# Routing logits issued as one block, and two of the last half's first four stores issued by GpSimd

## The chip, the cores and the metric

The kernel runs on one core of one Trainium2 chip. The time is the device time of one execution in microseconds (us); of several runs the median counts. The engines are called as in the profile: PE is TensorE (PEld its weight loads), DVE is VectorE, ACT is ScalarE, POOL is GpSimd, SP is SyncE. SP, ACT and POOL also issue the DMAs, each from its own queue and in the order of its program. A "q" behind an engine's name stands for its instruction queue. L12 is line 12 of the kernel.

## The reference

Three things are computed one after the other, all in float32.

1. A polysketch attention over 4 batches, 4 heads, 1088 positions and 32 features: queries and keys are mapped to 64 products of two 8-wide sketches, and the output is `num / den` with the sums over the keys.
2. A bridge turns the output into `x`, 4352 tokens by 128 features.
3. A Sinkhorn routing over 8 experts, each a two-layer network with 1024 hidden units:

```
logits = x @ w_gate                      # 4352 x 8
P = exp(logits - logits.max())
for _ in range(8):                       # rows, then columns
    P /= P.sum(1, keepdims=True) + 1e-09
    P /= P.sum(0, keepdims=True) + 1e-09
    P *= N / E
for e in range(E):
    h = relu(x @ w1[e])
    out += P[:, e:e+1] * (h @ w2[e])
```

## The kernel before

**Layout.** Tokens lie along the free axis: `xT` holds 128 features by 4352 tokens, in four batches of 1088. The experts' networks are the bulk of the work. A matrix product is cut into blocks of 64 rows and 64 columns, with sums and differences of blocks in place of some products, seven products where eight are plain. For that the second matrices `w2` of experts 1 to 7 are brought into seven derived blocks ("forms") in DRAM first.

**Phases.** First attention, batch by batch. Then the logits, the exponential and eight Sinkhorn rounds (`routing`). Neither fills PE, so the network of the first expert, which needs no weights `P` (they are applied to its outputs later), is worked off beside them: `first` (L763, product L770 and relu L772, DVE differences L785) and `into` (L824, second product L834), with copies of finished sums on ACT (L693 to L710). At the end of `routing` the transposed `P` goes to DRAM (`pT`, L622). Then comes the weighted phase (`weighted`, L1109) for the other experts: a row of `pT` is spread over the partitions (`load_weights`, L1058, DMA L1062), POOL multiplies `xT` by it (`weigh`, L1064, L1069), SP swaps the halves (L1072), POOL and DVE make the block sums (`sum_x`, L1074, L1077), the first matrices come with `load_raw` (L952, L958), the second ones with `load_second` (L965, L972 and L975), and PE runs first products (L1156) and second products (L1309) to the end.

**What sets the order.** The stretch around the change stands in a `manual_schedule` over DVE and PE alone: on these two the instructions come in the order of the program text. ACT's, POOL's and SP's order is the scheduler's choice, except for instructions pinned with `keep_in_program_order`, which keep their order among each other. `attention` and `routing` are generators that yield amounts of fill; the driver calls `fill(n)` with each, which runs that many steps of the first expert's network. The driver (L1640 to L1647) counts the yields of `routing` from `i = 0`: at the first it takes a step of `second_forms`, up to `i = 4` it fills the whole amount at once, and from `i = 5` on it fills twice half of it and takes a step of `second_forms` behind each half. Before, the yields are 5, 0.6, 0.6, 0.6, 2.2 and then 4.25 in each of the eight Sinkhorn rounds.

**The logits.** `logits(c)` (L493) issues, for chunk `c` of 512, 288 and 288 tokens of each batch, a 32-column product per batch (L497) into one PSUM bank; `logits_turned` (L503) lets DVE transpose the bank into `lgp` (L506). The maximum over all is taken on DVE (L585), turned by PE (L589), and ACT takes the exponential (L594).

**The second forms.** `second_forms` (L991) loads the raw matrices into buffers of the early phases, then in four stages for each expert 1 to 7: `begin` negates one half on ACT (L1015) and lets SP copy four parts to DRAM (L1016, L1018, L1020, L1022; the last two read the negated half); `add_first`, `add_second` and `add_third` are accumulating DMAs issued by POOL (L1025). All are pinned. When all is issued the early pools are closed (L1650), and the pool `late`, which holds the tiles of L1062, takes their place.

**The end.** The last group of tokens is finished in two halves by `finish_last` (L1525): for `u == 0` the sum is completed on DVE (L1510 to L1523) and transposed into a tile `r`, for `u == 1` the accumulator is transposed into a tile `yt` (both L1535). `store` (L727, DMA L736) writes a half with four DMAs of 32 partitions, dealt over the queues that it is given, in turn. POOL's last arithmetic is L1437; L1698 is the end of the program, with a DRAIN on each engine and a barrier.

Of the kernel before, what the change touches and what calls it, by code (L numbers as in the profile page):

```python
# [52 lines left out]
def kernel(  # L53
# [12 lines left out]
    nc = tc.nc  # L66
# [30 lines left out]
    def bank():  # L97
        return aps.tile([P, 512], F32, tag="a", name="a")
# [394 lines left out]
    def logits(c):  # L493
        lo, hi = chunks[c]
        pg = bank()[:, 0:hi - lo]
        for b in range(B):
            nc.tensor.matmul(pg[32 * b:32 * (b + 1)], wg, xT[:, b * S + lo:b * S + hi], start=True, stop=True,  # L497
                             tile_position=(0, 32 * b))
        lgs.append((c, pg))
# [3 lines left out]
    def logits_turned():  # L503
        c, pg = lgs.pop(0)
        lo, hi = chunks[c]
        nc.vector.transpose(out=lgp[:, lo // 32:hi // 32, :].rearrange("p a e -> p (a e)"), in_=pg)  # L506
# [69 lines left out]
    def routing():  # L576

        yield 5
        for c in range(len(chunks)):
            logits(c)  # L580
            yield 0.6
            logits_turned()
        lg = lgp[:, :, 0:E]
        mx = sk.tile([P, 1], F32, tag="mx", name="mx")
        nc.vector.tensor_reduce(out=mx, in_=lg, axis=AX.XY, op=Alu.max)  # L585
        yield 2.2
        pm = bank()[:, 0:P]
        for s in range(2):
            nc.tensor.matmul(pm[64 * s:64 * (s + 1)], mx.to_broadcast([P, 64]), ident, start=True, stop=True,  # L589
                             tile_position=(0, 64 * s))  # L590
        nc.vector.reduce_max(mx, pm, axis=AX.X)
        nc.vector.tensor_scalar(mx, mx, -1.0, 64 * math.log(2.0), op0=Alu.mult, op1=Alu.add)
        pw = p2s[0]
        nc.scalar.activation(out=pw[:, :, 0:E], in_=lg, func=Act.Exp, bias=mx[:, 0:1])  # L594

        step = 1.5 * 2.0 ** (23 - 149 + 64)
        nc.vector.tensor_scalar(pw[:, :, 0:E], pw[:, :, 0:E], step, step, op0=Alu.add, op1=Alu.subtract)
        for it in range(ITERS):
            rs = sk.tile([P, SA], F32, tag="rs", name="rs")
            nc.vector.reduce_sum(rs, pw, axis=AX.X)  # L600
            nc.vector.reciprocal(rs, rs)
            p1 = p1s[it % 2]
            nc.vector.scalar_tensor_tensor(p1[:, 0:SA], rs.unsqueeze(2).to_broadcast([P, SA, E]), UP,
                                           pw[:, :, 0:E], op0=Alu.mult, op1=Alu.mult)
            cs = sk.tile([P, E], F32, tag="cs", name="cs")
            nc.vector.reduce_sum(cs, p1.rearrange("p g e -> p e g"), axis=AX.X)
            yield 4.25
            pc = bank()[:, 0:E]
            for s in range(2):
                nc.tensor.matmul(pc[64 * s:64 * (s + 1)], ones[:, 0:64], cs, start=True, stop=True,  # L610
                                 tile_position=(0, 64 * s))
            cr = sk.tile([P, E], F32, tag="cr", name="cr")
            nc.vector.reciprocal(cr, pc)
            last = it == ITERS - 1
            pw = lgp if last else p2s[(it + 1) % 2]
            nc.vector.scalar_tensor_tensor(pw[:, :, 0:E], cr.unsqueeze(1).to_broadcast([P, SA, E]),
                                           float(N) / E * (1.0 if last else UP), p1[:, 0:SA],
                                           op0=Alu.mult, op1=Alu.mult)

        nc.vector.transpose(out=lgT.rearrange("p a s -> p (a s)"), in_=lgp.rearrange("p a e -> p (a e)"))  # L620
        for b in (1, 0, 2, 3):
            nc.sync.dma_start(out=pT[:, b * S:(b + 1) * S],  # L622
                                                  in_=lgT[32 * b:32 * b + E].rearrange("p a s -> p (a s)"))
# [99 lines left out]
    def one_store():  # L723
        if stores:
            stores.pop(0)()

    def store(yt, b0, b1, queues=(nc.sync,), put_off=False):  # L727
        first, k = b0, 0
        while b0 < b1:
            b, a = divmod(b0, SA)  # L730
            m = min(b1 - b0, SA - a)
            for r in range(4):
                to = AP(tensor=out.tensor, offset=out[b * S + a, 32 * r].offset, ap=[[SA * DM, 32], [DM, m], [1, 32]])
                from_ = yt[32 * r:32 * (r + 1), b0 - first:b0 - first + m, :]
                queue = queues[k % len(queues)]
                stores.append(lambda queue=queue, to=to, from_=from_: queue.dma_start(out=to, in_=from_))  # L736
                k += 1
            b0 += m
        while stores and not put_off:
            one_store()  # L740
# [368 lines left out]
    def weighted():  # L1109
# [170 lines left out]
        def seconds(t):  # L1280
# [33 lines left out]
            if g in whole and last:  # L1314
                begin_last(g)
                for u, cols in ((0, (0, n)), (1, (0, 128)), (1, (128, n))):
                    m = 2 * u + (cols[0] > 0)
                    for k, b in enumerate(((0, 2), (3, 1))[u]):
                        for r in range(2):
                            for half in range(2):  # L1320
                                nc.tensor.matmul(  # L1321
                                    acc[g][m][H2 * half:H2 * (half + 1), cols[0]:cols[1]],
                                    raw(half, k, r), flat(h[b], n)[:, r, cols[0]:cols[1]],
                                    start=False, stop=True, tile_position=(0, H2 * half),
                                    skip_group_check=True)
                    finish_last(g, u, cols)
                yield
                yield
                return
# [161 lines left out]
        def turned_room(k, n):  # L1491
            t = late[0].tile([P, NW], F32, tag="yt", name="yt", bufs=1)[:, 0:n] if k else room("r", n)
            return t.rearrange("p (b d) -> p b d", d=32)
# [9 lines left out]
        def last_of(g, u):  # L1503
            lo, n, es = wgroups[g]
            return lo + n * (1 - u), n

        def add_sum(g, m, u, cols):
            at, n = last_of(g, u)
            y = kept[0][:, at + cols[0]:at + cols[1]]
            nc.vector.tensor_tensor(y, acc[g][m][:, cols[0]:cols[1]], y, op=Alu.add)  # L1510
# [14 lines left out]
        def finish_last(g, u, cols):  # L1525
            at, n = last_of(g, u)
            if cols[0] == 0:
                ends[g, u] = turned_room(u, n)
            yt = ends[g, u]
            y = kept[0][:, at:at + n]  # L1530
            if u:
                y = acc[g][2 + (cols[0] > 0)][:, cols[0]:cols[1]]
            else:
                add_sum(g, 0, 0, cols)
            nc.vector.transpose(out=yt[:, cols[0] // 32:cols[1] // 32].rearrange("p b d -> p (b d)"), in_=y)  # L1535
            if cols[1] == n:
                store(yt, at // 32, (at + n) // 32, (nc.sync, nc.scalar))

        behind = (x for at in range(len(todo)) for x in seconds(at))
        for t in range(len(todo)):  # L1540
# [60 lines left out]
    with tc.manual_schedule(engines={engines.DVE, engines.PE}):  # L1601
# [38 lines left out]
        for i, n in enumerate(routing()):  # L1640
            if i == 0:
                next(made)
            for _ in range(2 if i > 4 else 0):
                fill(n / 2)
                next(made, None)
            if i < 5:
                fill(n)  # L1647
# [55 lines left out]
```

## Time and profile before

| | |
|---|---|
| median of 3 runs | 882.61 us (882.1 to 882.68) |
| profiled execution | 881.87 us |
| its span | 880.1 us |
| mean granted TensorE clock | 1.0 |
| PE busy | 874.7 us (99%) |
| DVE busy | 724.0 us (82%) |
| ACT busy | 386.8 us (44%) |
| POOL busy | 261.8 us (30%) |
| DMA | 149.06 MB, mean 169 GB/s |

The span is the time from the first to the last recorded instruction; the execution's own time lies 1.77 us above it. PE counts as busy while its pipelined matmuls are modelled to run. Idle time of an engine that others don't wait for costs nothing, so for DVE, ACT and POOL the timelines around a wait say more than these shares. In the rows below, a row of a timeline has start, duration, engine, line, operation, output and inputs, the count of instructions put together, and in brackets the idle time ahead of it with what ended it; a row of the chain of waits has start, duration and what stood on the chain.

### The profile page before, as it was taken

The numbers are of one execution on the slowest core, as the hardware profiler recorded it, in microseconds if no ns is written. First come the engines' busy times: TensorE is split into PE (matmuls) and PEld (weight loads), VectorE is DVE, ScalarE is ACT, GpSimd is POOL, SyncE is SP. The second block draws the span as 40 slices with busy tenths as digits, with TensorE's granted clock in tenths as the row PEclk, the third lists the DMA queues.
The fourth block names the chain that finished last, engine by engine and source line by source line (L and its number), as shares of the span: only waits on it lengthen the run. The fifth ranks groups of instructions, "written<-read, shape, count | busy, mean of one in ns | idle before, by whom it ended". The sixth has DMA issues, their size and how long they took to land.

```text
span 880.1 us, 26108 instructions
## 1 busy us (share of the span) xinstructions
PE 874.7 (99%) x10792; PEld 600.0 (68%) x10792; DVE 724.0 (82%) x982; ACT 386.8 (44%) x801; POOL 261.8 (30%) x254
## 2 busy tenths in 40 slices
PE   9999999999999999999999999999999999999998
PEld 6788656878775666666666666666555555557776
DVE  8699689978888877777887778888788888888897
ACT  3455557544444433333343333334343344444442
POOL 3131126354433323222222222221323323312431
PEclk9999999999999999999999999999999999999999
DMA  8888399796766554444435544434755557567662
GB/s 262 269 287 267 91 220 257 119 263 193 209 189 205 165 164 121 142 135 130 126 100 138 143 123 126 119 111 111 193 152 148 153 139 218 151 153 220 215 198 49
DMA packets 120887, 149.06 MB, mean 169 GB/s; under 512 B 52289, under 2 KB 79809, under 8 KB 120385
## 3 DMA queue, kind: packets, MB, share of 16 engines
q1 hardware_dynamic: 112656, 136.92, 54.8%
q0 software_dynamic: 6720, 10.19, 5.8%
q8 instruction: 85, 1.39, 0.6%
q10 hardware_dynamic: 1392, 0.28, 0.2%
q14 instruction: 34, 0.27, 0.1%
HBM read 104.86 MB, written 25.99 MB: 149 GB/s over the span
## 4 chain that ended last, share of the span: by engine, by line
PE 99%; DMA 0%; DVE 0%; SPq 0%; issue 0%; DVEq 0%
PE pair L1156 39%; PE s L1309 39%; PE a L770 9%; PE s L834 7%; PE a L336 1%; PE a L465 1%; DMA kx<-in_k_dram 0%; PE a L306 0%; PE s L375 0%; PE a L429 0%; PE s L395 0%; PE a L497 0%; PE s L1321 0%; PE a L375 0%; PE a L395 0%; PE a L610 0%
## 5 line engine op out<-in xcount | busy, mean ns | idle before, releaser
L1156 PE MATMUL pair<-xf,w1x 64*64 64x320 f32 (+3 forms) x4496 | 552.1, 466 | 0.0
L1309 PE MATMUL s<-hb,w 64*64 64x480 f32 (+3 forms) x2544 | 354.2, 466 | 0.0
L1156 PEld LDWEIGHTS pair<-xf,w1x 64*64 64x64 f32 x4496 | 258.7, 133 | 110.3 <-ACT hb L1169 0.9
L1172 DVE CUSTOM_DVE_ANT_0 hb<-pair,copies 128x960 f32<-128x960 f32 (+3 forms) x234 | 214.8, 918 | 100.7 <-PE pair L1156 89.7
L1309 PE MATMUL s<-hb,ws 64*64 64x480 f32 (+3 forms) x1888 | 274.5, 468 | 0.0
L1309 PEld LDWEIGHTS s<-hb,w 64*64 64x64 f32 x2544 | 153.1, 133 | 63.4 <-ACT turn L1362 0.4
L1309 PEld LDWEIGHTS s<-hb,ws 64*64 64x64 f32 x1888 | 115.0, 133 | 47.2 <-DVE hb L1221 0.6
L1069 POOL TENSOR_TENSOR xf<-xT,pb 128x960 f32<-128x960 f32 (+3 forms) x40 | 70.1, 1755 | 240.4 <-ACT turn L1362 184.1
L1077 POOL TENSOR_TENSOR xf<-xf 128x960 f32<-128x960 f32 (+3 forms) x39 | 68.4, 1753 | 225.3 <-ACT turn L1362 159.9
L1169 ACT ACTIVATE hb<-pair 128x640 f32<-128x640 f32 (+3 forms) x86 | 66.4, 772 | 148.4 <-PE pair L1156 148.4
L770 PE MATMUL a<-xT,w 128*64 128x416 f32 (+3 forms) x512 | 122.7, 464 | 0.0
L772 ACT ACTIVATE hb<-a 128x416 f32<-128x416 f32 (+3 forms) x128 | 59.5, 468 | 57.1 <-PE a L770 51.7
L1214 DVE TENSOR_TENSOR hb<-hb 128x960 f32<-128x960 f32 (+3 forms) x78 | 75.7, 971 | 7.5 <-PE pair L1156 0.5
L1362 ACT COPY turn<-s 128x1 f32<-128x1 f32 x134 | 20.9, 156 | 138.7 <-PE s L1309 138.7
L1221 DVE TENSOR_TENSOR hb<-hb 128x960 f32<-128x960 f32 (+3 forms) x78 | 72.4, 928 | 8.1 <-DVE hb L1218 0.9
L1217 DVE TENSOR_TENSOR hb<-hb 128x960 f32<-128x960 f32 (+3 forms) x78 | 76.4, 979 | 2.6 <-ACT hb L1169 0.8
L1250 ACT COPY copies<-pair 128x960 f32<-128x960 f32 (+3 forms) x78 | 59.8, 767 | 35.5 <-PE pair L1156 35.4
L1246 ACT COPY copies<-pair 128x960 f32<-128x960 f32 (+3 forms) x78 | 60.0, 769 | 33.1 <-PE pair L1156 33.1
L1241 ACT COPY copies<-pair 128x960 f32<-128x960 f32 (+3 forms) x78 | 59.8, 767 | 33.1 <-PE pair L1156 29.2
L834 PE MATMUL s<-hb,ws 128*64 128x416 f32 (+3 forms) x224 | 71.6, 474 | 0.0
L1218 DVE TENSOR_TENSOR hb<-hb 128x960 f32<-128x960 f32 (+3 forms) x78 | 71.4, 915 | 0.0
L770 PEld LDWEIGHTS a<-xT,w 128*64 128x64 f32 x512 | 54.5, 137 | 19.0 <-issue 7.2
(206 smaller groups left out, 662.4 us busy)
## 6 DMA issues: line engine op xcount, KB each, us to landing
w1x<-w1x SPq DMA_DIRECT2D x87, 256.0 KB, 4.0
w<-w2x SPq DMA_DIRECT2D x71, 256.0 KB, 3.1
ws<-w2x SPq DMA_DIRECT2D x35, 256.0 KB, 3.5
pb<-pT SPq DMA_DIRECT2D x14, 480.0 KB, 4.2
xf<-xf SPq DMA_DIRECT2D x28, 240.0 KB, 3.1
w1x<-w1x SPq DMA_DIRECT2D x7, 896.0 KB, 6.2
ws<-w2x SPq DMA_DIRECT2D x36, 128.0 KB, 3.4
pb<-pT SPq DMA_DIRECT2D x13, 320.0 KB, 4.4
```

The costliest lines, as they stand in the source:

```text
L770: nc.tensor.matmul(ph[sl], loaded_w[j][0][:, P * f + H2 * s:P * f + H2 * (s + 1)], xT[:, at + lo:at + hi], start=True, stop=True, tile_pos ...
L834: nc.tensor.matmul(sums[g][i][H2 * s:H2 * (s + 1)], w, x, start=c == 1, stop=c == per, tile_position=(0, H2 * s))
L1069: nc.gpsimd.tensor_tensor(xf[:, 0:2].rearrange("p b n -> p (b n)"), xT[:, lo:lo + 2 * n], weights.pop(i), op=Alu.mult)
L1077: nc.gpsimd.tensor_tensor(xf[:, 4:6], xf[:, 1:4:2], xf[:, 0:2], op=Alu.subtract)
L1156: nc.tensor.matmul(out[H2 * col:H2 * (col + 1), r], w1[rows, PLACE[form], o:o + H2], xf[rows, x], start=start, stop=stop, tile_position=(H ...
L1169: nc.scalar.activation(out=x, in_=y, func=Act.Relu)
L1172: nc.vector._custom_dve(TENSOR_ADD_SAT, out=flat(out, n), in0=x, in1=flat(y, n), s0=math.inf, s1=0.0)
L1214: nc.vector.tensor_tensor(ts[0], h[3], h[0], op=Alu.subtract)
L1217: nc.vector.tensor_tensor(ts[1], h[3], h[1], op=Alu.subtract)
L1218: nc.vector.tensor_tensor(ts[2], h[1], ts[0], op=Alu.subtract)
L1221: nc.vector.tensor_tensor(ts[3], h[2], ts[2], op=Alu.subtract)
L1309: nc.tensor.matmul(out_[H2 * half:H2 * (half + 1)], w[rows], flat(x, n)[rows, r], start=c == 1, stop=True, tile_position=(H2 * rho, H2 * h ...
```

## The change

Two places. In `routing` the three `logits` are issued one right behind the other; the transposes of the first two chunks follow at once, then the fill of 0.6, then the third transpose. The fill that stood between the chunks (0.6 each) is added to the one behind the maximum, so that the sum is as before (4.0 up to L589): 0.6 three times and 2.2 become 0.6 and 3.4. So `routing` yields three times instead of five ahead of the Sinkhorn rounds. In `finish_last` the four stores of the half `u == 0` are dealt over SP, ACT, POOL, POOL instead of SP, ACT, SP, ACT; those of `u == 1` stay. Lines behind L582 are two further down in the changed kernel.

```
@@ routing
         for c in range(len(chunks)):
             logits(c)
-            yield 0.6
-            logits_turned()
+        logits_turned()
+        logits_turned()
+        yield 0.6
+        logits_turned()
         lg = lgp[:, :, 0:E]
         mx = sk.tile([P, 1], F32, tag="mx", name="mx")
         nc.vector.tensor_reduce(out=mx, in_=lg, axis=AX.XY, op=Alu.max)
-        yield 2.2
+        yield 3.4
@@ finish_last
             if cols[1] == n:
-                store(yt, at // 32, (at + n) // 32, (nc.sync, nc.scalar))
+                store(yt, at // 32, (at + n) // 32, (nc.sync, nc.scalar) if u else (nc.sync, nc.scalar, nc.gpsimd, nc.gpsimd))
```

## The prediction

> **What bounds the kernel now.** I read the page first, then the chain of waits.
>
> ```profile
> span 880.1 us, 26108 instructions
> PE 874.7 (99%) x10792; PEld 600.0 (68%) x10792; DVE 724.0 (82%) x982; ACT 386.8 (44%) x801; POOL 261.8 (30%) x254
> PE 99%; DMA 0%; DVE 0%; SPq 0%; issue 0%; DVEq 0%
> ```
>
> PE is busy in 874.7 of 880.1 us and makes up 99% of the chain that ended last. So there is next to nothing to win: a gain needs fewer PE microseconds or a shorter tail behind PE. There is much to lose: whatever makes PE wait is added in full. I therefore read three places: PE around the logits, the stretch between the logits and the first weighted product (which engine waits for what), and the last ten microseconds. The profiled execution took 881.87 us, 1.77 more than its span; the median of the three runs shown is 882.61, so I add 0.74 to whatever the sum gives.
>
> **Part 1: the logits on PE.** The timeline of PE (start, duration, line, operation, count):
>
> ```profile
> 107.60 0.51 PE L834 MATMUL s<-hb,ws 128*64 128x416 f32 x1
> 108.04 1.06 PE L497 MATMUL a<-xT,wg 128*32 128x512 f32 x8
> 109.04 0.92 PE L770 MATMUL a<-xT,w 128*64 128x416 f32 x4
> 109.79 0.87 PE L834 MATMUL s<-hb,w 128*64 128x416 f32 x4
> 110.58 1.18 PE L497 MATMUL a<-xT,wg 128*32 128x288 f32 x16
> 111.69 0.92 PE L770 MATMUL a<-xT,w 128*64 128x416 f32 x4
> ```
>
> and two rows of the chain:
>
> ```profile
> 169.82 0.35 PE a L770 x2
> 187.38 5.54 PE pair L1156 x80
> ```
>
> Two 64-column matmuls side by side with 416 columns take 0.35 us. By columns, a wave of four 32-column logit matmuls takes 0.43 at 512 and 0.24 at 288. From 107.60 to 111.69 are 4.09 us; the work in them is 0.35 (the last L834) + 0.86 (chunk 0, two waves) + 0.70 + 0.70 (the FFN step between) + 0.97 (chunks 1 and 2, four waves) = 3.58. The 0.51 left are four changes between 32- and 64-column tiles, 0.13 each at most (some of it is the half step by which the L834 are offset). The FFN step now comes behind all three chunks, so two changes go: **-0.2 us**, bounds 0 and -0.5. The fill time taken from here is put behind the reduction (2.2 to 3.4), so PE's work up to the maximum stays the same.
>
> DVE's turns of the logits, before:
>
> ```profile
> 111.29 1.07 DVE L506 STREAM_TRANSPOSE kT<-a 128x512 f32<-128x512 f32 x2
> 112.76 0.47 DVE L506 STREAM_TRANSPOSE kT<-a 128x288 f32<-128x288 f32 x1
> ```
>
> The first two, 1.07 us together, now stand ahead of two L785 and an L683 instead of behind them, where the logits of chunks 0 and 1 are complete at about 109.0 and 109.6. PE would wait if it wanted a bank that DVE hasn't read, or the relu that L785 makes: both come a step (four L770, four L834: 1.4 us) later, and each turn takes half a microsecond. I cost it at nothing; uncovered, it would be the 1.07.
>
> **Part 2: what the change moves without naming it.** The driver of `routing` counts its yields: from the sixth on (`i > 4`) it fills in two halves and takes a step of `second_forms` behind each. Before, five yields stand ahead of the Sinkhorn rounds (5, three of 0.6, 2.2), so the forms begin in the first round. Now there are three (5, 0.6, 3.4), so `i` is 3 and 4 in the first two rounds, and the forms begin **two rounds later**; ten steps at two a round still fit into the six rounds left. The order of the changed program's instructions agrees: ahead of ACT's first negation (L1015) now stand seven relus (L772), a group of part copies (L693 to L710) and two relus more, where it was two relus behind the exponential. Two rounds by L610, a product that each has once, are 12.9 us:
>
> ```profile
> 122.44 0.29 PE L610 MATMUL a<-cs,ones 128*64 128x8 f32 x4
> 135.30 0.23 PE L610 MATMUL a<-cs,ones 128*64 128x8 f32 x2
> ```
>
> and by ACT's order the new place of the first negation is the one right behind the two relus at 133.87:
>
> ```profile
> 120.32 0.62 ACT L1015 ACTIVATE halves<-halves 128x512 f32<-128x512 f32 x1
> 133.87 0.93 ACT L772 ACTIVATE hb<-a 128x416 f32<-128x416 f32 x2
> 140.21 0.62 ACT L1015 ACTIVATE v<-v 128x512 f32<-128x512 f32 x1
> ```
>
> So the first negation goes from 120.32 to about 134, **13 to 14 us later**, and the last from 140.21 to about 154. Behind it hang SP's queue, in order, and POOL's accumulate DMAs (L1025), in order:
>
> ```profile
> 117.94 1.08 SPq L1018 DMA_DIRECT2D w2x<-halves  x1
> 120.96 0.37 SPq L1020 DMA_DIRECT2D w2x<-halves  x1
> 151.34 0.74 SPq L1022 DMA_DIRECT2D w2x<-v  x1
> 172.06 1.35 SPq L622 DMA_DIRECT2D pT<-qT  x4
> 175.75 0.83 SPq L1062 DMA_DIRECT2D pb<-pT  x2
> 181.32 1.17 SPq L1072 DMA_DIRECT2D xf<-xf  x2
> ```
>
> ```profile
> 123.41 2.19 POOL L1025 DMA_DIRECT2D w2x<-halves  x2 [22.19 <-DMA w2x<-halves]
> 165.26 0.89 POOL L1025 DMA_DIRECT2D w2x<-v  x1 [0.90 <-DMA w2x<-v]
> 179.76 1.54 POOL L1069 TENSOR_TENSOR xf<-xT,pb 128x640 f32<-128x640 f32 x1 [9.97 <-DMA pb<-pT]
> ```
>
> SP's L1020 waits for the first negation: behind 117.94 it sits until 120.96, which is 120.32 + 0.62. The chain ends with the accumulate of form 7 issued at 165.26; it reads a buffer of the early pools, and L1062, the first load into the late pool that takes their place, waits for it. Landing times of L1025 (minimum, median, maximum):
>
> ```profile
> DMA to landing us min/median/max: 3.4/7.1/10.3
> ```
>
> At the minimum it lands at 168.7. L1062 was issued at 175.75 on account of L622, so the chain had 7.1 us of **cover**. PE's first weighted product (L1156, 187.38) needs L1069, and the second, one step of 0.54 later at 187.92, needs the swap DMAs of L1072, issued from 181.32 to 182.5, which land
>
> ```profile
> DMA to landing us min/median/max: 2.6/2.6/2.6
> ```
>
> after issue: the path from the issue of L1062 to this product is 8.8 us long (175.75 to 184.5). So there is a second cover of 187.92 - 184.5 = 3.4 us. Does the chain shift by the full two rounds? The row of the stretch from 118 to 160 says what limits it:
>
> ```profile
> 118.00:160.00 42.00, 42.00 (x269) 28.01 (x267) 38.24 (x75) 28.04 (x59) 20.77 (x21) 1.00 1.12 242
> ```
>
> (the last two columns are DMA share and GB/s). From 118 to 160 the transfers fill the engines, and each form is issued two rounds late besides, so the chain runs faster only where emptier engines let its tail catch up. I take a shift of 13.5 us, between 12 and 15. Form 7 lands at 182.2, L1062 goes out at 182.7 (I allow 0.5 for the wait itself), and the second product can start at 191.5 to 191.9. PE is there at 187.92 - 0.2 = 187.7. **Stall: +4.0 us**; 2.3 at a shift of 12, 6 at 15, and nothing if the chain makes up 4 us of its delay. The next loads are pushed by the same 7 us, of which PE's own delay of 4 covers the larger part; the rest of 3 us they have:
>
> ```profile
> 182.60 1.01 SPq L972 DMA_DIRECT2D w<-w2x  x2
> 192.92 0.61 PE s L1309 x8
> ```
>
> L972 goes out 10.3 us ahead of the L1309 that reads it. So I add nothing more for them. From there the loop is PE bound as before and gives nothing back.
>
> **Part 3: the end.** Two of the four stores of the first half (`r`, L736) go from SP and ACT to POOL. The tail before, one row each of the timelines of SP (twice), DVE and POOL, and the landing times of all L736:
>
> ```profile
> 875.63 0.82 SPq L736 DMA_DIRECT2D out_dram<-r  x2
> 876.54 0.91 SPq L736 DMA_DIRECT2D out_dram<-yt  x2
> ```
>
> ```profile
> 876.06 0.28 DVE L1535 STREAM_TRANSPOSE yt<-s 128x96 f32<-128x96 f32 x1 [0.26 <-PE s L1321]
> ```
>
> ```profile
> 872.96 0.66 POOL L1437 TENSOR_TENSOR w<-w,m 64x224 f32<-64x224 f32 x1
> ```
>
> ```profile
> DMA to landing us min/median/max: 1.6/1.7/1.8
> ```
>
> The last transpose ends at 876.34 and the second half's first store goes out at 876.54, behind the two `r` stores: 0.2 us to save, if those stores alone set the end. What POOL itself does at the end stands in the view of the kernel's last line, L1698:
>
> ```profile
> L1698 POOLq DRAIN  x3: 46/102/5527, 872.9 to 879.8; - x3
> L1698 SPq DRAIN  x3: 7/7/7, 879.3 to 879.6; - x3
> ```
>
> POOL's first drain starts at 872.9 and takes 5.53 us: it ends at 878.4, 4.8 us behind the end of L1437 (873.6), though POOL has nothing left to do. No other engine has this: SP's take 7 ns. Now it is hidden, with 0.9 us to spare, because SP's first drain, the last to come, is at 879.3. In the changed kernel POOL's stores stand ahead of the drain. They wait for the `r` transpose, as the store at 875.63 does, and take on POOL what plain copies from POOL took at L489 (issue about 0.56 us each), with landings of
>
> ```profile
> DMA to landing us min/median/max: 2.4/2.5/2.6
> ```
>
> The second ends issuing at about 876.75 and lands by 878.8, no later than the `yt` stores now, the last of which goes out at about 877.0 and lands 1.6 to 1.8 us later; at L1025's fastest, 3.4, it would land at 879.6. The drain then ends at 876.75 + 4.8 = 881.6 instead of 878.4, and the barrier behind it goes from 879.3 to 881.6: **+2.3 us**, and the 0.2 of part 3 is hidden. Bounds: -0.2 if the drain's length belongs to a moment and not to what precedes it, +3 if it grows with the two stores.
>
> The Trainium skill, "DMA: Bandwidth & Descriptors", section "SWDGE vs HWDGE vs iDMA", says that plain transfers go to SP or ACT and only accumulating, casting or irregular ones to GpSimd: it speaks against this edit. By the fixed 2.0 us of its section "Anatomy of one DMA" the estimate for the second POOL store would be landed by about 878.7, and the end would not move; neither section has a price for the drain, which is what I count.
>
> **Sum.** -0.2 + 4.0 + 2.3 = +6.1 on 881.87, so 888.0; with 0.74, **888.7 us**.
>
> **The rivals.**
> - *Stall, but the drain stays hidden* (0.20): 881.87 - 0.2 - 0.2 + 4.0 + 0.74 = 886.2. For it: the profile doesn't say what the drain waits for. Against it: it starts the moment POOL is free, and nothing else ends at 878.4.
> - *Drain, but the forms catch up* (0.15): a shift under 10 us stays under 7.1 + 3.4 us of cover less the 0.5; some rest of the stall, 0.3, gives 881.87 - 0.2 + 0.3 + 2.3 + 0.74 = 885.0. For it: with the first negations late, the early transfers run in emptier engines.
> - *Not slower* (0.05): the cover at the start of the weighted phase swallows the delay of the forms. It decides at the same 10 us of shift, and needs the drain hidden as well; then only the two savings are left: 881.87 - 0.4 + 0.74 = 882.2, within the bound of no change. More than 0.4 us can't be won, since PE's other work is the same.
> - *The forms collide* (0.08): the last accumulate now runs beside L622 and lands at the slow end, 10.3 instead of 3.4; L1062 goes 5 to 7 us later still: +5 on the sum, 893.7.
>
> **How the numbers follow.** The forecast (stall and drain) has 0.52. Its own range, by the bounds of the shift, is 887.0 to 890.7. The range for 8 in 10 takes in the rival without the drain and most of the one without the stall: 884.3 to 890.6. 0.2% is 1.8 us, about what a measurement of this kernel can tell from no change. Faster by more than that: 0.03, for no row gives more than 0.4; within: 0.05; slower: 0.92.
>
> **What would show it.** Changes of tile near 108 to 111: two, not four. No step of the forms in the first two Sinkhorn rounds, the first negation at about 134 and the last at 154; the accumulate of form 7 near 179; L1062 at about 182 and released by that DMA; a gap on PE between the first and the second weighted product near 188 to 192, four microseconds long; POOL's long drain starting behind the `r` stores and ending at the span's end less 0.7. I am wrong if L1062 goes out near 176, if PE's busy share stays as it is, or if POOL's drain is short.

## The result and the profile after

The changed kernel takes 891.77 us in the median of 4 runs (891.44 to 892.77), the kernel before 882.36 (881.54 to 882.68): +9.4 us, ratio 1.011 with a 95% interval of 1.0092 to 1.0127. The forecast was 888.7, +6.1, with a range that ended at 890.6. The profiled execution of the changed kernel took 891.44 us with a span of 889.7. From its page:

```profile
span 889.7 us, 26109 instructions
PE 876.2 (98%) x10792; PEld 601.7 (68%) x10792; DVE 724.2 (81%) x982; ACT 387.2 (44%) x801; POOL 262.7 (30%) x256
PE 96%; DMA 2%; DVE 0%; POOL 0%; issue 0%; POOLq 0%; SPq 0%; DVEq 0%; ACT 0%; ACTq 0%
```

PE is busy 1.5 us longer with the same 10792 instructions, and the span grew by 9.6: PE stands still for longer, and something made the same matmuls slower. The three places that the prediction named show it one after the other. First PE around the logits:

```profile
107.82 0.51 PE L836 MATMUL s<-hb,ws 128*64 128x416 f32 x1
108.27 2.04 PE L497 MATMUL a<-xT,wg 128*32 128x512 f32 x24
110.23 0.92 PE L772 MATMUL a<-xT,w 128*64 128x416 f32 x4
110.98 0.87 PE L836 MATMUL s<-hb,w 128*64 128x416 f32 x4
111.68 0.87 PE L772 MATMUL a<-xT,w 128*64 128x416 f32 x4
```

One block of 24. From the last L836 ahead of it to the second L772 behind it are 3.86 us, where the same work took 4.09: 0.23 won, as forecast. Next the forms and the first weighted load, from the timelines of SP and POOL:

```profile
117.79 1.01 SPq L1020 DMA_DIRECT2D w2x<-halves  x1
134.27 0.37 SPq L1022 DMA_DIRECT2D w2x<-halves  x1
181.92 0.83 SPq L1064 DMA_DIRECT2D pb<-pT  x2
188.81 1.17 SPq L1074 DMA_DIRECT2D xf<-xf  x2
```

```profile
177.89 0.89 POOL L1027 DMA_DIRECT2D w2x<-v  x1 [0.83 <-DMA w2x<-v]
187.26 1.53 POOL L1071 TENSOR_TENSOR xf<-xT,pb 128x640 f32<-128x640 f32 x1 [4.74 <-PE s L836]
```

SP stands from 118.8 to 134.27, until the first negation is done, and the accumulate of form 7 comes at 177.89 instead of 165.26, 12.6 us later. L1064 (L1062 before) goes out at 181.92 instead of 175.75. The bracket at L1071 names PE, whose matmuls end every 0.35 us; the load that L1071 needs, the first `pb`, landed 5.0 us behind its issue (3.7 before), just ahead of it. PE at that place, and its granted clock by stretches of 1 us (the third column from the right, ahead of DMA share and GB/s):

```profile
190.66 1.35 PE L1158 MATMUL pair<-xf,w1x 64*64 64x320 f32 x8 [3.46 <-DMA w1x<-in_moe_w_dram]
192.87 6.49 PE L1158 MATMUL pair<-xf,w1x 64*64 64x320 f32 x72 [0.86 <-DMA xf<-xf]
```

```profile
192.00:193.00 1.00, 0.14 (x5) 0.14 (x6) 0.00 (x0) 0.00 (x0) 1.00 (x2) 0.63 1.01 373
193.00:194.00 1.00, 1.00 (x10) 0.62 (x14) 0.00 (x0) 0.00 (x0) 0.90 (x2) 0.50 0.92 320
...
195.00:196.00 1.00, 1.00 (x16) 0.68 (x12) 0.00 (x0) 0.05 (x1) 0.00 (x0) 0.66 0.98 199
196.00:197.00 1.00, 1.00 (x22) 0.57 (x18) 0.10 (x1) 0.70 (x1) 0.00 (x0) 1.00 0.95 261
```

The brackets are the two waits, 3.46 us ahead of the first product and 0.86 ahead of the second. The first product waited for its own weights, the load L960 behind L1064 in SP's queue, which landed 7.1 to 7.4 us after issue where it had been 5.4 to 5.5; the second waited for the halves that L1074 swaps. The second product starts at 192.87, where it was 187.92: **+4.95 us**. Behind it the clock reads 0.50, and the 72 matmuls take 6.49 us; before, 80 took 5.54, so 72 took 4.99: **+1.5 us**. Last, the end: POOL's stores, the last transpose, and the drains.

```profile
882.58 1.32 POOL L738 DMA_DIRECT2D out_dram<-r  x2 [2.29 <-DVE yt L1537]
```

```profile
882.73 0.28 DVE L1537 STREAM_TRANSPOSE yt<-s 128x96 f32<-128x96 f32 x1 [0.26 <-PE s L1323]
```

```profile
L1700 POOLq DRAIN  x3: 46/102/5820, 883.1 to 889.4; - x3
L1700 SPq DRAIN  x3: 7/7/7, 886.1 to 889.1; - x3
```

POOL's long drain starts at 883.1 and ends at 888.9; SP is done at 886.1 and waits for it. From the end of the last transpose to the end of the span are now 6.7 us (883.01 to 889.7) where there were 3.76 (876.34 to 880.1): **+2.9 us**. The parts 4.95 (in which the 0.2 won at the logits is contained), 1.5 and 2.9 make 9.35 of the span's 9.6; the rest is spread over the weighted phase.

### The profile page after: what moved, and what is told of

Read it like the earlier page. It is cut to its first block, busy times and chain, and to the rows that moved or that the text cites. A ratio compares the mean times of both kernels' runs of the same rounds, so it can differ in the third digit from the quotient of the medians.

```text
span 889.7 us, 26109 instructions
## 1 busy us (share of the span) xinstructions
PE 876.2 (98%) x10792; PEld 601.7 (68%) x10792; DVE 724.2 (81%) x982; ACT 387.2 (44%) x801; POOL 262.7 (30%) x256
## 4 chain that ended last, share of the span: by engine, by line
PE 96%; DMA 2%; DVE 0%; POOL 0%; issue 0%; POOLq 0%; SPq 0%; DVEq 0%; ACT 0%; ACTq 0%
PE pair L1158 39%; PE s L1311 38%; PE a L772 9%; PE s L836 7%; DMA qx<-in_q_dram 1%; PE a L465 1%; PE a L336 1%; DMA v<-in_v_dram 0%; DMA xf<-xf 0%; PE a L429 0%; PE a L306 0%; PE s L395 0%; DMA raw<-in_S_dram 0%; PE a L497 0%; POOL xf L1071 0%; DVE kT L289 0%
## 5 line engine op out<-in xcount | busy, mean ns | idle before, releaser
L1071 POOL TENSOR_TENSOR xf<-xT,pb 128x960 f32<-128x960 f32 (+3 forms) x40 | 70.5, 1763 | 234.4 <-ACT turn L1364 182.8
L772 PE MATMUL a<-xT,w 128*64 128x416 f32 (+3 forms) x512 | 121.7, 464 | 0.0
L836 PE MATMUL s<-hb,ws 128*64 128x416 f32 (+3 forms) x224 | 70.9, 474 | 0.0
L772 PEld LDWEIGHTS a<-xT,w 128*64 128x64 f32 x512 | 52.1, 137 | 23.0 <-issue 11.0
```

Of the source, the lines that this page charges most:

```text
L772: nc.tensor.matmul(ph[sl], loaded_w[j][0][:, P * f + H2 * s:P * f + H2 * (s + 1)], xT[:, at + lo:at + hi], start=True, stop=True, tile_pos ...
L836: nc.tensor.matmul(sums[g][i][H2 * s:H2 * (s + 1)], w, x, start=c == 1, stop=c == per, tile_position=(0, H2 * s))
L1071: nc.gpsimd.tensor_tensor(xf[:, 0:2].rearrange("p b n -> p (b n)"), xT[:, lo:lo + 2 * n], weights.pop(i), op=Alu.mult)
```

## The experiments

The theory, from the two traces: three independent things happen. The block of logits wins a little; the forms begun two Sinkhorn rounds late make PE wait and then run at half the clock; the two stores on POOL push its drain out. The rivals: that the block costs by itself; that it takes block and late forms together; that the stores count only by their landing.

**Each part alone.** Four kernels on one chip. The two stores on the kernel before:

```
-  store(yt, at // 32, (at + n) // 32, (nc.sync, nc.scalar))
+  store(yt, at // 32, (at + n) // 32, (nc.sync, nc.scalar) if u else (nc.sync, nc.scalar, nc.gpsimd, nc.gpsimd))
```

> The kernel before with the two GpSimd stores alone. Theory (POOL's long drain starts behind its last instruction and is pushed out by the stores): +2.9 us on before, as the tail of the changed kernel grew from 3.76 us behind the last transpose to 6.7; POOL's drain about 5.8 us long, starting at about 876.4, the last thing ahead of the barrier. Rival (the stores matter only by when they land, 1.6 to 2.2 us after issue): no change within 0.3 us, and POOL's drain ends before SP's.

Measured: 884.94 against 882.31, ratio 1.0028 (1.0017 to 1.004), +2.6. The drains of this kernel:

```profile
L1698 POOLq DRAIN  x3: 46/102/5815, 876.4 to 882.7; - x3
L1698 SPq DRAIN  x3: 7/7/7, 879.5 to 882.4; - x3
```

POOL's first drain ends at 882.2, SP's first is at 879.5 as before, and the stores themselves have landed long before. The rival is out.

The logits in one block, with the forms where they were:

```
-            for _ in range(2 if i > 4 else 0):
+            for _ in range(2 if i > 2 else 0):
...
-            if i < 5:
+            if i < 3:
```

(on the changed kernel, with the stores on SP and ACT).

> The changed kernel with its stores as before and the driver's bounds lowered by two (i > 2 and i < 3), so that the forms begin in the first Sinkhorn round as before; the logits stay in one block. Theory (the block itself is harmless and all of the loss at the start of the weighted phase comes from the late forms): -0.3 us on before, no idle time of PE ahead of the first weighted product. Rival (the block, with DVE's first two turns ahead of its other work, costs time by itself): 2 us or more slower than before.

Measured: 882.43 against 882.31, ratio 1.0002 (0.9993 to 1.0011). PE goes from the first network to the products without a gap:

```profile
187.35 5.61 PE L1158 MATMUL pair<-xf,w1x 64*64 64x320 f32 x80
```

The block costs nothing; the 0.3 that it should win are below what this run can tell.

The late forms alone, on the kernel before: `i > 4` to `i > 6`, and `i < 5` to `i < 7`.

> The kernel before, logits and stores as before, with the driver's bounds raised by two (i > 6 and i < 7), so that the forms begin in the third Sinkhorn round. Theory: +6.5 us on before: 5.0 of idle PE between the last product of the first network and the second weighted product, and 1.5 at half the granted clock behind it. Rival (the forms alone aren't it; the block of logits is needed for the stall): within 1 us of before.

Measured: 889.54, ratio 1.0083 (1.0068 to 1.0098), +7.2. PE:

```profile
190.84 1.09 PE L1156 MATMUL pair<-xf,w1x 64*64 64x320 f32 x8 [2.94 <-DMA w1x<-in_moe_w_dram]
193.10 2.51 PE L1156 MATMUL pair<-xf,w1x 64*64 64x320 f32 x16 [1.17 <-DMA xf<-xf]
```

The same two waits, without any change at the logits or the stores (the view ends at 195 us, so its last row counts only 16 matmuls). The chain that ended last goes from the last accumulate that reads an early buffer, through the load and the swap, to PE; its four longest pieces are:

```profile
178.30 3.45 DMA w2x<-v
182.25 5.70 DMA pb<-pT
190.42 2.64 DMA xf<-xf
193.10 7.83 PE pair L1156 x72
```

By this chain the load waits for that accumulate, as the prediction has it. The 72 matmuls take 7.83 us here, 2.8 more than the 4.99 of the kernel before. The three parts alone make +0.1, +7.2 and +2.6: 9.9 to the 9.4 of the whole.

One round late (`i > 5`, `i < 6`):

> The kernel before with the forms beginning one Sinkhorn round late (i > 5 and i < 6). Theory with the cover of the prediction (a shift under 9.7 us costs nothing): a shift of 6.5 us, the load of the first weights goes out at about 176 as before, and the time is within 0.5 us of before. Rival (no such cover, the stall grows in step with the shift): +3 us.

Measured: 883.33, ratio 1.0009 (1.0 to 1.0018), +1.0.

```profile
178.64 0.83 SPq L1062 DMA_DIRECT2D pb<-pT  x2
```

```profile
188.12 0.77 PE L1156 MATMUL pair<-xf,w1x 64*64 64x320 f32 x8
189.91 5.17 PE L1156 MATMUL pair<-xf,w1x 64*64 64x320 f32 x72 [1.02 <-DMA xf<-xf]
```

A cover there is, but the expectation of it was wrong in two places. The chain ended later than one round would have it: the accumulate of form 7 went out at 175.07, 9.8 us late, not 6.5, after 3.6 us of waiting that the trace puts down to the transfer of `pT`. And from the issue of L1062 to the second product are 11.3 us instead of 8.8. The load is issued 2.9 us late and the path is 2.5 longer; less the second cover of 3.4 that makes 2.0, by which the second product starts later than before (189.91 for 187.92). The wait of 1.0 us left the clock at full: 72 matmuls in 5.17.

**The drain.** A small copy on POOL in place of the stores:

```
                 store(yt, at // 32, (at + n) // 32, (nc.sync, nc.scalar))
+                if not u:
+                    nc.gpsimd.tensor_copy(y[:, 0:32], yt[:, 0, 0:32])
```

> The kernel before, all stores on SP and ACT as before, with one small copy on GpSimd (128x32) behind the first half's last transpose; its result is read by nobody. Theory (the long drain follows whatever POOL does last): the drain starts at about 875.7 and takes about 4.8 us behind the copy, ends at 880.5 and costs 1.3 us on before. Rival (it is the stores' DMAs, issued late by POOL, that the drain waits for): no change within 0.3 us.

Measured: 883.86 against 882.35, ratio 1.0019 (1.001 to 1.0028), +1.5.

```profile
L1700 POOLq DRAIN  x3: 46/102/5052, 876.0 to 881.6; - x3
```

No DMA of POOL is near, and the drain still takes 5.05 us behind a copy of 0.21 that runs inside it. So it is whatever POOL does last that the drain follows. What it is made of shows where POOL issues more DMAs long before:

```
+            if 8 <= t < 28:
+                for _ in range(2):
+                    nc.gpsimd.dma_start(out=spare[0:16], in_=ones[0:16, 0:8])
```

> The kernel before with 40 small additional DMAs issued by GpSimd in the middle of the weighted phase, two at each of 20 steps, to a buffer that nobody reads; 98 GpSimd DMAs in all instead of 58. Theory (the drain's length grows with the number of DMAs that POOL has issued before, 0.083 us each, as 58 gave 4.83 us and 60 gave 4.98): the long drain takes about 8.8 us in all, ends at about 881.7 and costs 2.4 us on before. Rival (its length is fixed, or depends only on DMAs in flight): 5.5 us as before and no change beyond 0.5 us.

Measured: 885.21 against 882.35, ratio 1.0036 (1.0022 to 1.0049), +2.9.

```profile
L1702 POOLq DRAIN  x3: 46/102/8792, 872.9 to 882.2; - x3
```

The drain grew from 5.53 to 8.79 us, 3.26 for 40 DMAs: 0.082 each. From the end of POOL's last instruction to the end of the drain are 4.83 us with 58 DMAs (before, and with the copy), 4.98 with 60 (the stores alone, and the changed kernel), 8.10 with 98: 0.083 for each in every case, though the 40 additional ones are small. The additional transfers are issued in the middle of the weighted phase; none is in flight at the end.

If that is a debt, it can be paid earlier. On the changed kernel with early forms:

```
         for t in range(len(todo)):
+            if t == 30:
+                nc.gpsimd.drain()
```

> The changed kernel with the forms begun in the first Sinkhorn round as before (i > 2, i < 3), the two GpSimd stores kept, and one additional drain of GpSimd in the middle of the weighted phase, in one of its idle stretches of 8 us. Theory (the drain works off a debt of 0.083 us for each DMA that POOL issued since the last one): the additional drain takes about 4.8 us beside PE's work, the one at the end 0.2 us for two DMAs and is hidden; the time is that of before or up to 0.5 us less, 881.9. Rival (the end's drain takes its 5 us whatever came before): +2.6 on before, 885.0.

Measured: 882.29 against 882.06, ratio 1.0004 (0.9996 to 1.0012): the loss of the stores is gone, and no version here is measurably faster than the kernel before. The additional drain, the last POOL instruction of the stretch in which it runs, and the drain at the end:

```profile
L1544 POOLq DRAIN  x1: 7950/7950/7950, 462.6 to 462.6; - x1
```

```profile
464.80 0.94 POOL L1101 TENSOR_TENSOR kept<-kept,pk 128x352 f32<-128x352 f32 x1
```

```profile
L1702 POOLq DRAIN  x3: 51/102/2522, 876.0 to 879.6; - x3
```

The additional drain ends at 470.56, 4.83 us behind the end of L1101 (465.74), with 58 DMAs issued before it: the same 4.83 as at the end of the kernel before, more than 280 us after the last of these DMAs. So the length follows the count, and not the place in the program. The end's drain fell from 5.82 to 2.52 us. It isn't the expected 0.2 behind the second store (which ended issuing at 876.84): 1.7 are left. It ends at 878.53, 0.13 behind the landing of that store at 878.40; that it waits for this landing is a guess from one run.

**The clock.** Additional matmuls in PE's wait, ahead of the first product of the changed kernel, with results that are overwritten:

```
+        for k in range(14):
+            for s in (0, 1):
+                nc.tensor.matmul(pairs[1][H2 * s:H2 * (s + 1), 1, 0:416], ones[:, 0:H2], xT[:, 0:416],
+                                 start=True, stop=True, tile_position=(0, H2 * s), skip_group_check=True)
```

> The changed kernel with 28 additional matmuls (64 columns, 416 wide, about 4.9 us) ahead of the first weighted product, whose results are overwritten: they fill PE's wait. Theory (1.5 us of the loss are PE running at half the granted clock after the wait, because it had stood still): the clock stays at 1.0 from 192 to 196, the 72 matmuls of L1158 behind the second product take 5.0 us instead of 6.5, and the time is 1.5 us under the changed kernel's, about 890.3. Rival (the slow stretch comes from what the products wait for, the weights and the halves coming in): as the changed kernel, 891.8, or longer.

Measured: 894.65, ratio 1.014 (1.0126 to 1.0154): slower, by an error of the experiment. The trace has 56 matmul records for the 28, two passes each; they took 10 us and pushed the products to 196.5. With half of them (`range(7)`):

> As the run with 28 additional matmuls, with 14, since each of them turned out to be two passes and 28 took 10 us instead of 4.9. Theory (1.5 us of the loss or more are PE at half the granted clock after its wait): 14 take 5.0 us and end at about 192.2, the second product starts at about 192.9 as in the changed kernel, the clock stays at 1.0, the 72 matmuls behind it take 5.1 us instead of 6.5, and the time is 1.4 us or more under the changed kernel's: 890.3 or less. Rival (the slow stretch comes from what the products wait for): as the changed kernel, 891.8.

Measured: 891.01, ratio 1.0098 (1.0084 to 1.0113). To compare on one chip, the changed kernel and this one once more:

> The changed kernel once more, as the partner of the next run on the same chip. PE waits for the second product until about 193 and then runs one or two windows of about 3.4 us at half the granted clock: 891 to 893, with a spread of more than 1 us from run to run.

> The changed kernel with 14 additional matmuls in PE's wait, once more beside the changed kernel. Theory (the half clock is part of the loss): 1.3 us or more under its partner. Rival (PE would have waited as long with or without, and what is late sets the pace): no difference within 0.5 us.

Measured: 891.74 for the changed kernel (891.58 to 894.29), 891.36 with the matmuls (890.68 to 891.64). The products of the changed kernel again, and of the second run with 14 matmuls:

```profile
189.71 2.10 PE L1158 MATMUL pair<-xf,w1x 64*64 64x320 f32 x8 [2.43 <-DMA w1x<-in_moe_w_dram]
192.58 7.35 PE L1158 MATMUL pair<-xf,w1x 64*64 64x320 f32 x72 [0.76 <-DMA xf<-xf]
```

```profile
192.08 1.20 PE L1158 MATMUL pair<-xf,w1x 64*64 64x320 f32 x8
194.40 5.17 PE L1158 MATMUL pair<-xf,w1x 64*64 64x320 f32 x72 [1.11 <-DMA xf<-xf]
```

What the expectation says of the clock came true: with PE kept busy the 72 matmuls take 5.17 us, twice, and not 6.49 or 7.35. (With the forms one round late they took the same 5.17 behind a wait. So 0.2 over the 4.99 of the kernel before come with a wait even at the full clock, and the half clock cost 1.3 and 2.2 us in the two profiles of the changed kernel.) What it says of the time didn't: 0.4 us and 0.8 us (each against 891.8), inside the intervals. The loads went out later in these two runs (L1064 at 182.67 and 182.87; in the changed kernel 181.92 and 181.19), before any added matmul ran, so the products began 0.6 to 1.8 us later. Why the chain of forms ends up to 1.7 us later in one run than in another isn't settled, nor how much of the total the clock costs.

**What makes the path long.** The changed kernel without `add_third` of experts 6 and 7, which leaves their forms incomplete:

```
-            add(f[:, F3], f[:, F1])
+            if e < 6:
+                add(f[:, F3], f[:, F1])
```

> The changed kernel without the last accumulating DMAs (add_third) of experts 6 and 7, so that part of their second matrices' forms is left incomplete; the load of the first weights still waits for add_second of expert 7. Theory (from its issue to the swapped halves the path takes 10.9 us instead of 8.8 because it runs beside the last accumulates): the path shrinks to about 9, PE waits some 1.5 to 2 us less, and the time falls to about 889 to 890. Rival (the loads of L960 and L1064 slow each other, whatever POOL issues): as the changed kernel, 891.8.

Measured: 890.17, ratio 1.0092 (1.0078 to 1.0105), 1.6 under the changed kernel and near what was expected, but with intervals that overlap. In the profile the load goes out at 182.49 and the second product starts at 191.84: 9.35 us, where it is 10.8 to 11.5 in the six other traces with late accumulates that show it. So the last accumulates do lengthen the path, by this one trace without them. The profiled execution is the slowest of its four (891.65): what it won on the path it lost to the clock, with 8.10 us for the 72 matmuls. The windows from the issue of the load on, the changed kernel and this one:

```profile
181.92:190.70 8.78, 5.32 (x33) 2.27 (x29) 5.59 (x9) 3.02 (x6) 2.87 (x3) 1.00 0.88 177
```

```profile
182.50:191.20 8.70, 6.66 (x37) 2.62 (x33) 5.94 (x9) 2.99 (x6) 4.13 (x4) 0.99 0.70 174
```

The DMA share is 0.88 against 0.70 (0.70 also in the kernel before, from 175.75 to 184.5) at about the same GB/s. Over the whole path this doesn't hold everywhere: with the forms two rounds late alone the share is 0.75. It is clearer in the first 4 us behind the issue of the load: 0.75 to 0.94 in the seven traces with late accumulates, 0.51 in this one and 0.46 before, at 136 to 163 GB/s in all. That the accumulates hold the engines with little data to show for it is read from this, not tested further. Nor is it the same transfer each time that comes late: the first `pb` landed 5.0 and 5.7 us after issue in the changed kernel and with the forms two rounds late, but 3.7, as before, with the forms one round late, where the swap took 5.0.

## Why the prediction was wrong

**The direction was right, and most of the places.** The logits: -0.23 for -0.2, and nothing on DVE. The driver's count: no step of the forms in the first two rounds, the first negation at 133.6 (forecast 134), the last at 154.7 (154). The shift: 12.6 us for 13.5, L1064 at 181.92 for the 182.7 of the sum. POOL's drain is the last thing ahead of the barrier. The parts alone confirm each, but for the 0.2 of the logits, which is too small for them. One place was off: the gap was forecast between the first and the second weighted product, and 3.46 us of it came ahead of the first. The prediction let that product wait for L1069 alone; it waited for its weights, whose load goes out behind L1064.

**The step that failed is "Stall: +4.0 us".** Two terms of it were wrong. The path of 8.8 us from L1062 to the second product was taken from the kernel before, where POOL had issued the last accumulate 6.8 us ahead of the load; in the changed kernel it is 0.2 us ahead (181.71), the path runs beside the accumulates and took 10.95, and 10.9 and 11.3 with the forms late alone and one round late. The smaller shift gave back 0.8. So the wait was about 5.1 (4.95 and the 0.2 that PE came earlier). And a term was missing: the slower matmuls behind the wait, 1.5 us in this profile (1.3 by the half clock), 2.4 and 2.8 in others. The stall term is 6.6 us in the trace for 4.0, and 7.2 with the forms late alone.

The Trainium skill, "TensorE: Matmul & The Clock Gate", section "Part 1: The HAM clock gate", says that an idle window of about 3.4 us halves the clock and that it takes a busy stretch of about that length to get it back; the window runs freely, so that the cost varies from run to run. The traces agree with the length: by the shares of the stretches above, the clock stood at half from about 192.3 to 195.7, 3.4 us; with the forms late alone from about 191.8 to 198.6, two such windows; and a wait of 1.0 us left it alone. They differ in what halves it: PE need not be idle for 3.4 us at a stretch. The longest idle stretch ahead of the fall was 3.46 us in the changed kernel, 2.43 in its second profile and only 1.59 without the last accumulates (187.65 to 189.24, then eight matmuls, then 1.08 idle), and the clock fell in all three, each time after the first eight matmuls had begun. The forecast had a gap of four microseconds and did not ask what PE's clock would do in it.

**"+2.3" for the drain was 2.9** (2.6 alone). The mechanism was right, the size off by 0.6: with the stores alone POOL's second one ended issuing at 877.2, not 876.75, since the two start 0.3 us behind SP's and take 0.66 us each, not 0.56; and two more DMAs add 0.15 to the drain (4.98 for 4.83).

**The range** ended at 890.6 because the bounds of the stall were those of the shift alone, 2.3 to 6 (its own sum gives 5.3 to 5.7 at a shift of 15). The path was held fixed in both ends. The rival of colliding transfers (893.7, 0.08) is nearer by its number, but not by its mechanism: it has the accumulate land late and the load go out 5 to 7 us later, and the load went out 0.8 us earlier than forecast. What came late were the transfers behind the load.

## What to carry to other kernels

Where a driver counts the yields of a generator, a change to the yields moves whatever the count starts; here a block of three groups of matmuls moved seven unrelated DMA chains by two rounds. When a wait of PE is forecast, ask for the clock behind it (two waits of 3.5 and 0.9 us with eight matmuls between them halved it here, and even two of 1.6 and 1.1; one of 1.0 us did not), and time a path that moves by the traffic where it will run, not where it ran. Before an engine gets a last instruction, look at what it still does at the end: a drain that was hidden can become the end of the kernel.

## What the runs showed of the hardware

GpSimd's drain at the end of the program took 0.083 us for each DMA that it had issued, 4.8 us for 58 and 8.1 for 98, counted from its last instruction and however early these were; a drain in the middle of the kernel took the same 4.8 us and cut the last one from 5.8 to 2.5. Behind two waits of PE with eight matmuls between them the clock stayed at half for one or for two windows of 3.4 us, so that the same 72 matmuls took 6.49 and 7.35 us in two runs of the changed kernel, and 7.83 and 8.10 in two variants, for 4.99 at the full clock without a wait and 5.17 behind one.
